# Zero products, landing times and the last step in a kernel whose order is written out

## The chip, the cores and the metric

The kernel runs on one core of a Trainium2 chip. The time is that of the device, in microseconds (us), for one execution; before the change the median of three runs is 809.19 us (808.46 to 811.43).

## The reference

Attention within chunks of 64 tokens (4 batches, 8 heads, 576 tokens, head size 64), and behind it two feed-forward layers over the same 2304 tokens of 512 values, each with 2048 hidden values. The first layer squares its rectified hidden values and applies a scale and an offset; the second is a softplus. All weights of the layers are given as 64-bit floats and are used as 32-bit ones.

```python
scores = scale * np.matmul(q_c, k_c.transpose(0, 1, 2, 4, 3))      # chunks of 64
attn = np.exp(scores - np.max(scores, axis=-1, keepdims=True))
attn = attn / (np.sum(attn, axis=-1, keepdims=True) + 1e-09)
x = np.matmul(attn, v_c)                                           # to 2304 x 512
h = x @ moe_w_in;  r = np.maximum(h, 0.0)
x = (moe_s * (r * r) + moe_b) @ moe_w_out
h = x @ moe2_w_in
return (np.maximum(h, 0.0) + np.log1p(np.exp(-np.abs(h)))) @ moe2_w_out
```

## The kernel before, in words

Attention is done in 18 tiles of 128 tokens (`attention`): scores on TensorE, maximum on VectorE, exponentials on ScalarE, division on GpSimd, a transpose and the product with v on TensorE.

Each of the four matrix products of the layers is computed by a scheme of seven products of half-size blocks in place of eight, with sums of blocks ("forms") made by VectorE and GpSimd. A number is split into a high part, rounded by ScalarE (line 1090), and a low part, the rest, by VectorE (line 1099); a product is then three matmuls (high by high, high by low, low by high) of 128 x 128 weights with 384 columns. All of them have one shape, so a block's product is six matmuls.

A phase is one layer. In its first multiplication (`quad`, matmuls at line 1509) a unit is 256 hidden values by a group of 768 tokens: seven products into four PSUM banks, seeds copied from one bank to the next by ScalarE (line 1531), the nonlinear function on ScalarE (line 1542), and six results stored to DRAM (`summed`). In the second multiplication (`second_by_blocks`, matmuls at line 1952) these are loaded again (`features`, line 1722), split (`divided`), and multiplied with the forms of the second weights. Those forms are made during the first multiplication (`weights2`), spilled to DRAM in eight groups (`spilled`), and loaded by `weights` (line 1663) before their step. One step of the second multiplication is one of the seven products for one of the three groups of tokens: eight products of six matmuls into two banks, three to one bank (`d` = 0) and three to the other (`d` = 1), then `read_out` adds both into the running sums. The last step of the second phase writes the output.

The 32-bit weights come from 64-bit words by integer operations on VectorE and ScalarE (`convert`, lines 956 to 1057).

PSUM has eight banks here: A (2), S (3), at (3). SBUF holds rings of buffers, among them `go` for hidden values on their way to DRAM.

The order of the work is written out. Every operation has a rank in the table `PLAN`, by the name of its turn ("second0 0 1 2 0" is phase 0, product 1, group 2, part 0), with V for VectorE and G for GpSimd where an operation has a choice. `Work.order` (line 669) walks the ranks with assumed durations, one queue to each engine, and gives each operation a planned start and end: a load lands after its bytes at `BYTES` and a constant, `LOAD`, `FIRST` (attention) or `STORE`. The real program is emitted in the order of planned starts; each engine runs its own list in that order and waits on the chip for what it needs. The planned times themselves enter the program at one place only, `warmed` (line 732): where TensorE has a planned gap before an operation, it emits matmuls with an all-zero operand (`nought`, `idle`, line 2075) into a bank that nobody uses. Before, that bank is S2, and no zero product is emitted once S2 is taken for the first time.

All DMAs are issued from one queue (SP, line 918; the loads of attention at line 1286), in the order of the list: a DMA that waits holds those behind it.

Of the kernel before, what the change touches and what calls it, by code (L numbers as in the profile page):

```python
# [19 lines left out]
P = 128  # L20
# [7 lines left out]
NF = NM // 2  # L28
# [48 lines left out]
    "": "0 837 21",  # L77
    "attention 0": "1 2 3 31 12 19 23 25 - 38 42 48 52V 58 64V 68 74",
    "attention 1": "5 6 7 27 22 28 34 41 - 55 60 66 76V 84 106 109 93 95 98 100 108 112",
    "attention 2": "8 9 10 13 37 43 49 56 - 72 75 81 89 107 113 115 121",  # L80
    "attention 3": "20 26 29 85 54 61 70 77 - 90 94 99 104 111 120 128 124 126 132G 130 141 149",
    "attention 4": "33 45 47 91 71 79 86 92 - 110 117 127 131V 135 152 146 156",
    "attention 5": "44 62 69 114 96 102 119 122 - 134 139 147 151 155 164 168 161 166 171 172 175 181",
    "attention 6": "59 63 65 143 88 97 105 133 138 145 153 158 165 174 202 196 205",
    "attention 7": "78 80 82 150 129 142 154 157 163 178 185 190 194 198 206 227 208 210 222G 216G 237 248",
    "attention 8": "101 123 140 184 162 173 177 180 - 197 201 209 215 221 231 229 239",
    "attention 9": "103 116 118 188 169 186 192 199 203 217 226 232 242 249 273 283 256 261 277G 266G 290 305",
    "attention 10": "136 144 148 244 204 213 220 225 230 246 251 259 267 271 279 284 289",
    "attention 11": "170 179 182 240 228 234 245 247 - 264 272 282 288 294 307 314 313 318 323G 321G 380 385",
    "attention 12": "176 183 214 257 243 252 258 262 270 280 285 291 297 302 311",  # L90
    "attention 13": "211 218 238 298 265 275 278 281 286 301 310 333 336 344 359",
    "attention 14": "235 253 255 312 287 295 300 315 - 327 331 340 346 350 363",
    "attention 15": "250 260 263 316 317 322 324 328 332 341 349 356 366 372 383",
    "attention 16": "274 296 304 353 326 334 338 343 347 354 360 368 373 376 386",
    "attention 17": "293 306 309 358 335 345 352 355 361 364 371 375 378 381 392V",
    "held 6": "400 407 390 397 367 402 417 413 411 445 420 442",
    "held 7": "414 427 389 394 391G 415 438 431G 424 449 453 460",
    "held 8": "408 423 395 399 404 412 435 429 418 421 450 456",
    "weights1 0 0": "4 14V 15 18 16 17 24 11 32V 36 39 35 40 46 53 57 30 51G 50 67 73 83",
    "quad0 0 0": "187 191 193 200V 212 233 224 254 268 308 348 236 269 299 276 325 398 320 330 339 369 365 401 342G 377 382 362 406 388",  # L100
    "weights1 0 1": "87 137 160 167 159 189 195 125 219 223 303 241 292 319 351 379 207G 337G 329 357 370 374",
    "quad0 1 0": "387 393 396 405 410 422 419 425 432 437 441 416 426 434 430 439 448 443 457 465 455 458 452 468 470 472 477 474 480",
    "quad0 0 1": "403 433 436 444 447 459 463 467 475 484 492V 461 473 489V 471 502 509 485 493 499 496 500 514 503 506 519 508 512 540",
    "quad0 1 1": "454 476 481 488 491 507 513 518 523 528 534 498 522 531 511 561 571 533 541 545 537 544 572 554 557 562 569 574 566",
    "quad0 0 2": "505 524 527 535 539 551 548 559 564 583 586 546 565 592 563 588 599 570 585 591V 590 594 605 598 604 612 603 609 616",
    "quad0 1 2": "553 568 573 581 584 597 593 602 610 622 632 579 615 620V 608 650 655V 613 625 634 703 624 659 637 639 644G 675 643 649",
    "weights1 0 2": "384 428 446 462 440 451 466 409 469 478 483 479 482 487 575 580 516 497 529 549G 578 582",
    "quad0 2 0": "589 617 621 629 635 640 642 647 653 660 696 638 648 651V 652 657 691 669 679 683 699 673 715 686G 708 724 695 712 866",
    "quad0 2 1": "627 654 656 662 665 672 678 682 690 735 737 689 704 711 676 685 716 694 729 742V 740 717 722 747 753G 761G 756 774 777",
    "quad0 2 2": "595 692 701 709 713 723 728 732 754 748 772 707 731 767V 743 757 768 758 765 770 795 771 791 773 783 818 862 788 848",  # L110
    "weights1 0 3": "611 661V 664 668 663 667 671 645 674V 680 687 681 684 693 698 705 677G 700 697 702 706 710",
    "quad0 3 0": "719 733 738 745 752 766 762 775 781 787 810V 764 776 789V 793 812 826 785 796 799 822 842 831 803 821 830G 807 834 846",
    "quad0 3 1": "727 750 780 794 804 816 813 823 832 861 886 811 819 838 855 902 910V 845 852 856 899 897 939 869 890 895 888 911 919",
    "quad0 3 2": "769 784 800 806 817 825 835 851 863 857 877V 829 864 884 836 854 878 881 889 892 891 967 893 898G 903G 920 916 907 924",
    "weights1 0 4": "726 779V 782 790 786 792 797 763 802 809 814 808 815 824 844 850 805 827 839 843 849 853",
    "quad0 4 0": "860 870 887 896 900 912 917 921 930 935 943 874 909 933 960 982 988 934 941 946V 948 1040 992 953 958G 969 956 980 974",
    "quad0 4 1": "868 875 894 901 904 915 927 947 959 954 957 913 926 931 928 938 945 968 978 1005 976 962 970 1018 1025G 1032 1027 1031 1043",
    "quad0 4 2": "905 929 940 949 952 966 963 975 984 993 997 981 1002 1011 987 1020 1028 991 1000 1007 1001 1033 1096 1021 1035 1041G 1066 1076 1069",
    "weights1 0 5": "859 914V 918 922 925 932 936 908 942V 951 961 944 950 965 973 986 955 979 972G 983 985 989",
    "quad0 5 0": "996 1010 1015 1026V 1029 1036 1039 1044 1052 1047 1048 1022 1038 1068 1050 1060 1109 1057 1065 1072 1054 1073 1112 1078G 1089 1092 1100 1093 1102",  # L120
    "quad0 5 1": "1003 1013 1034 1063 1071 1088 1083 1104 1120 1116 1124 1079 1086 1099 1097 1144 1149V 1126 1136 1140V 1162 1115 1167 1145 1156 1161 1151 1159 1203",
    "quad0 5 2": "1009 1042 1045 1055 1064 1074 1080 1084 1108 1127 1134 1090 1111 1122 1107 1138 1163 1114 1148 1154 1147 1125 1190 1157 1164G 1176 1169 1217 1210",
    "weights1 0 6": "999 1049V 1053 1058 1056 1059 1061 1037 1067V 1077 1082 1070 1075 1085 1091 1105 1087 1098 1095 1103 1106 1110",
    "quad0 6 2": "1119 1129 1132 1141 1146 1155 1165 1174 1186 1192 1196V 1179 1188 1195 1158 1170 1183 1191 1199 1202 1201 1207 1214 1206 1213 1224 1220 1237 1228",
    "weights1 0 7": "1171 1204V 1208 1211 1209 1215 1222 1187 1225 1230 1235 1229 1232 1238 1242 1249 1226 1245 1243 1247 1250 1254",
    "quad0 7 2": "1259 1267 1273 1280V 1284 1293 1297 1310 1319 1332 1337V 1279 1289 1303V 1296 1308 1324V 1323 1329 1342V 1361 1307 1327 1356 1358 1362G 1359 1363 1367",
    "quad0 6 0": "1153 1160 1168 1175 1184 1193 1200 1205 1219 1257 1272 1218 1227 1248 1255 1262 1270 1246 1260 1264V 1278 1268 1276 1269 1275 1283 1274 1281 1287",
    "quad0 7 0": "1302 1311 1317 1325 1328 1340 1336 1349 1360 1390 1394 1357 1366 1371V 1353 1393 1402 1364 1391 1400 1407 1384 1405 1406 1413 1425 1410 1416 1443",
    "quad0 6 1": "1137 1173 1197 1216 1223 1233 1236 1240 1252 1298 1330V 1212 1295 1300 1251 1334 1354 1266 1301 1314 1346 1304 1370 1318G 1333 1350 1412 1386 1381",
    "quad0 7 1": "1291 1316 1335 1339 1341 1372 1355 1379 1395 1428 1434 1399 1432 1439 1404 1440 1462 1411 1437 1453V 1445 1442 1473 1460 1461 1469 1464 1475 1470",  # L130
    "weights2 0 0": "464 490 495 504 494 501 510 486 515 520 525 521 526 532 536 538 542 543G 550 552 556",
    "weights2 0 1": "517 547 555 558 560 567 577 530 587V 601 606 596 600 614 618 623 607 626 636 633 630",
    "weights2 0 2": "576 619 641 646 628 631 658 670 714 720 725 718 721 730 734 736 666 739 746 744 749",
# [5 lines left out]
    "second 0": "1377 1375 1378 1418 1419 1433",  # L139
    "weights 0 1": "1343 1345 1368 1392 1382 1398 1408 1427 1430 1435",  # L140
    "second0 0 1 2 0": "1331 1385 1389 1396",
    "second1 0 1 2 1": "1415",
    "second2 0 1 2 2": "1388 1414 1421",
    "second3 0 1 2 3": "1426",
    "second0 0 1 2 4": "1373 1403 1420 1431",
# [2005 lines left out]
```

## Time and profile before

| what | us |
|---|---|
| three runs | 808.46, 809.19, 811.43 |
| profiled execution | 808.3 |
| its span, first to last instruction | 806.5 |
| TensorE busy with matmuls | 775.9 |
| VectorE busy | 669.8 |
| ScalarE busy | 544.2 |
| GpSimd busy | 116.9 |

The profile shows one execution. PE is TensorE, DVE VectorE, ACT ScalarE, POOL GpSimd, SPq the queue that issues DMAs. Busy time counts from a matmul's start to its modelled end. "PEclk" is the granted clock of TensorE as a share of 2.4 GHz: 0.50 is 1.2 GHz. L2075 are the zero products, L1509 and L1952 the matmuls of the first and the second multiplication. Attention takes the time to about 80 us, the first phase that to about 447 us.

### The profile page before, as it was taken

Reading aid. Unit: us, or ns where it says so; the run is one execution under the profiler, and the core shown is the slowest. Engines: PE = TensorE matmul, PEld = TensorE weight load, DVE = VectorE, ACT = ScalarE, POOL = GpSimd, SP = SyncE. Lnnn points to the kernel's source line nnn. Section 1 sums busy time; section 2 is a strip of 40 time slices with the busy share of each in tenths; the row PEclk is TensorE's granted clock in tenths of the full one; section 3 lists DMA queues with packets and bytes.
Section 4 is the critical chain, followed back from the end, with each engine's and each line's share of the span. In section 5 each row is a group of like instructions: output and inputs, shape, how many; then the busy total and the mean of one; then the engine's idle time right before and its main releaser. Section 6 shows DMA issues by size and latency. Waiting matters only on the chain.

```text
span 806.5 us, 14244 instructions
## 1 busy us (share of the span) xinstructions
PE 775.9 (96%) x4994; PEld 751.0 (93%) x4994; DVE 669.8 (83%) x1193; ACT 544.2 (67%) x1106; POOL 116.9 (14%) x115
## 2 busy tenths in 40 slices
PE   7898899999997999999999999999999999999998
PEld 5687799999996999999999899999999999999997
DVE  5998988998998799898999989999754688666754
ACT  5889897898987687766677865655555455454432
POOL 3355101113112000000001211101022131000000
PEclk8999999999999899999999999999999999999999
DMA  6765478899899989788884068987678987667554
GB/s 235 263 199 174 156 270 260 274 298 313 301 313 320 310 304 329 250 266 288 316 282 159 23 224 271 296 287 257 228 254 283 345 331 239 218 247 243 195 190 177
DMA packets 93658, 205.43 MB, mean 255 GB/s; under 512 B 10001, under 2 KB 64273, under 8 KB 92689
## 3 DMA queue, kind: packets, MB, share of 16 engines
q1 hardware_dynamic: 93584, 204.51, 74.4%
q8 instruction: 39, 0.64, 0.3%
q14 instruction: 35, 0.28, 0.1%
HBM read 128.45 MB, written 76.02 MB: 254 GB/s over the span
## 4 chain that ended last, share of the span: by engine, by line
PE 70%; ACT 9%; DVE 9%; DMA 7%; issue 3%; SPq 1%; POOL 0%; DVEq 0%; ACTq 0%; POOLq 0%
PE at L1509 18%; PE S L1952 12%; PE at L1952 12%; PE S L1509 10%; PE A L1952 7%; PE A L1509 7%; ACT operands L1090 4%; DVE operands L1099 3%; DMA last<-summed 3%; DVE mem L1077 2%; DMA summed<-mem 1%; DMA mem<-summed 1%; DVE last L1077 1%; ACT last L1346 1%; ACT mem L1542 1%
## 5 line engine op out<-in xcount | busy, mean ns | idle before, releaser
L1952 PE MATMUL S<-operands 128*128 128x384 f32 (+1 forms) x768 | 177.2, 337 | 4.5 <-ACT mem L1542 2.8
L1952 PE MATMUL at<-operands 128*128 128x384 f32 (+1 forms) x768 | 175.1, 335 | 0.0
L1099 DVE TENSOR_TENSOR operands<-mem,operands 128x768 fp32r<-128x768 f32 (+2 forms) x147 | 133.2, 925 | 41.2 <-ACT operands L1090 40.7
L1090 ACT CAST operands<-mem 128x768 fp32r<-128x768 f32 (+3 forms) x150 | 115.1, 793 | 70.0 <-PE at L1952 40.6
L1090 ACT CAST operands<-last 128x768 fp32r<-128x768 f32 (+2 forms) x136 | 103.0, 781 | 70.6 <-PE at L1952 33.1
L1952 PEld LDWEIGHTS S<-operands 128*128 128x128 f32 x768 | 136.6, 188 | 7.6 <-DVE operands L1099 4.0
L1077 DVE TENSOR_TENSOR mem<-mem 128x256 f32<-128x256 f32 (+1 forms) x258 | 123.4, 498 | 22.1 <-POOL mem L1077 7.0
L1077 POOL TENSOR_TENSOR mem<-mem 128x256 f32<-128x256 f32 (+1 forms) x72 | 74.3, 1036 | 446.4 <-DVE mem L1077 131.4
L1099 DVE TENSOR_TENSOR operands<-last,operands 128x768 fp32r<-128x768 f32 (+2 forms) x135 | 119.8, 910 | 22.2 <-ACT operands L1090 21.7
L1952 PEld LDWEIGHTS at<-operands 128*128 128x128 f32 x768 | 137.5, 188 | 0.0
L1509 PE MATMUL at<-operands 128*128 128x384 f32 x624 | 120.9, 337 | 4.7 <-ACT S L1531 2.0
L1509 PEld LDWEIGHTS at<-operands 128*128 128x128 f32 x624 | 108.7, 188 | 8.1 <-ACT S L1531 3.4
L1952 PE MATMUL A<-operands 128*128 128x384 f32 (+1 forms) x480 | 89.7, 337 | 1.7 <-DVE operands L1099 1.1
L1952 PEld LDWEIGHTS A<-operands 128*128 128x128 f32 x480 | 83.8, 188 | 3.2 <-DVE operands L1099 2.4
L1509 PE MATMUL S<-operands 128*128 128x384 f32 x420 | 84.3, 340 | 0.0
L1509 PEld LDWEIGHTS S<-operands 128*128 128x128 f32 x420 | 75.3, 192 | 0.4 <-issue 0.2
L1509 PE MATMUL at<-last,operands 128*128 128x384 f32 x336 | 67.8, 339 | 0.0
L1542 ACT ACTIVATE mem<-S 128x384 f32<-128x384 f32 x104 | 50.6, 491 | 24.7 <-PE S L1509 13.3
L1509 PE MATMUL A<-operands 128*128 128x384 f32 x300 | 60.8, 340 | 4.3 <-ACT mem L899 2.7
L969 ACT ACTIVATE mem<-mem 128x512 f32<-128x512 int32 x88 | 55.6, 632 | 8.9 <-DVE mem L960 8.1
L1509 PEld LDWEIGHTS at<-last,operands 128*128 128x128 f32 x336 | 59.5, 188 | 0.3
L1509 PEld LDWEIGHTS A<-operands 128*128 128x128 f32 x300 | 52.0, 188 | 7.2 <-ACT mem L899 3.3
(108 smaller groups left out, 927.3 us busy)
## 6 DMA issues: line engine op xcount, KB each, us to landing
summed<-mem SPq DMA_DIRECT2D x288, 192.0 KB, 3.0
mem<-in_w_dram SPq DMA_DIRECT2D x64, 512.0 KB, 4.7
last<-summed SPq DMA_DIRECT2D x40, 768.0 KB, 5.5
mem<-summed SPq DMA_DIRECT2D x20, 768.0 KB, 5.9
last<-summed SPq DMA_DIRECT2D x28, 384.0 KB, 3.9
last<-in_qk_dram SPq DMA_DIRECT2D x36, 256.0 KB, 3.8
forms<-mem SPq DMA_DIRECT2D x16, 512.0 KB, 4.2
mem<-summed SPq DMA_DIRECT2D x20, 384.0 KB, 6.5
```

Of the source, the lines that this page charges most:

```text
L969: return lambda e: nc.scalar.activation(out=out(), in_=in_(), func=AF.Prelu, scale=scale, bias=bias, alpha=alpha)
L1077: lambda e: on(e).tensor_tensor(out=out(), in0=x(), in1=y(), op=op or ALU.subtract),
L1090: lambda e: nc.scalar.copy(out=hi().bitcast(F32R), in_=x()),
L1099: lambda e: on(e).tensor_tensor(out=lo().bitcast(F32R), in0=x(), in1=hi(), op=ALU.subtract),
L1346: nc.scalar.activation(out=of("e")[:, h * D : (h + 1) * D], in_=at(sc)[:, h * D : (h + 1) * D], func=AF.Exp, scale=SCALE, bias=mx[:, h, 1: ...
L1509: nc.tensor.matmul(acc(dst)().rearrange("p (u c) -> p u c", u=GROUP), l[a], r[c], start=start and kk == 0 and x == 0, stop=kk == 1 and x == 2,
L1542: lambda e: nc.scalar.activation(out=at(go), in_=acc(place)(), func=AF.Softplus if ph else AF.Relu),
L1952: nc.tensor.matmul(at(accs[d])[:, :width], l[a], r[c], start=i == 0 and y == 0 and not seeds, stop=i == NF - 1 and y == 2, skip_group_chec ...
```

## The change

It has five parts. `warmed` looks at every gap of TensorE in the whole program: up to 30 us planned time as before (with at least two zero products before the first operation and four before the second), later only where the planned gap is 1.3 us or more; the bank is the one whose last use ended earliest, and there are none if that was less than 0.5 us before the gap. `FIRST`, `LOAD`, `STORE` and `BYTES` are changed, and the first weights load counts as one of the `FIRST` kind; the table `PLAN` is new in 500 of its lines. A load of spilled weight forms depends on those groups alone that it reads (in the first phase a load takes four of the eight; in the second it takes all). The last step of the second phase does its eight products for `d` = 0 and for `d` = 1 as separate operations of three matmuls, which share their split features (`cut_of`); so `last_of` holds an operation for each `d`, on which `read_out` depends.

```diff
-    "weights 0 1": "1343 1345 1368 1392 1382 1398 1408 1427 1430 1435",
+    "weights 0 1": "1326 1343 1371 1374 1376 1386 1404 1416 1420 1432",
...
-    "sums2 1 2 1": "3595 3597 3594 3596",
+    "second0 1 2 1 0 1": "3564",
...
+    "second3 1 2 1 7 1": "3596",
+    "sums2 1 2 1": "3604 3605 3599 3601",
...
-    STORE, LOAD, FIRST = 2.3, 2.2, 2.9
-    BYTES, TURN = 360e3, 0.6
+    STORE, LOAD, FIRST = 2.7, 2.5, 3.3
+    BYTES, TURN = 357e3, 0.6
...
-        op.lag = self.FIRST if self.part == "attention" else self.LOAD
+        op.lag = self.FIRST if self.part == "attention" or self.turn == "weights1 0 0" else self.LOAD
...
+    EARLY, LONG = 30.0, 1.3
+    FIRST_GAPS = 2, 4
+
+    def warmed(self, done, emit):
+
+        used = {(k, x): [] for k, n in (("S", 3), ("A", 2), ("at", 3)) for x in range(n)}
         for op in done:
-            unused = unused and all((u.kind, u.index) != (kind, index) for u in op.takes)
-            if op.on == "PE" and unused:
+            for u in op.takes:
+                if u.kind in self.BANKS:
+                    used[u.kind, u.index].append((op.start, u.until))
+        t, at, out = 0.0, 0, []
+        for op in done:
+            if op.on == "PE":
                 spare = self.SPARE[op.start < self.CROWDED]
-                for x in range(int((op.start - t - spare) / self.IDLE) if t else 2):
-                    out.append(Op({"PE": self.IDLE}, 0, [], [], [], emit, 0))
+                n = int((op.start - t - spare) / self.IDLE) if t else 0
+                n = max(n, self.FIRST_GAPS[at]) if at < len(self.FIRST_GAPS) else n
+                at += 1
+                if op.start > self.EARLY and op.start - t < self.LONG:
+                    n = 0
+                past = {k: max([b for a, b in v if a <= op.start], default=0.0) for k, v in used.items()}
+                bank = min(past, key=past.get)
+                if past[bank] > t - 0.5:
+                    n = 0
+                for x in range(n):
+                    out.append(Op({"PE": self.IDLE}, 0, [], [], [], lambda e, bank=bank: emit(e, bank), 0))
...
-                        [o for i in range(NF) for o in spilled[ph, i]]
+                        [o for i in range(y * m, y * m + m) for o in spilled[ph, i]]
...
+            elif ph and n == order[-1] and j == groups[2]:
+                products = [(n, i, (d,)) for d in range(2) for i in range(NF)]
+                cut_of = {}
...
+                if ds == (1,):
+                    work.begin(f"second{i % 4}", ph, n, j, i, 1)
+                    pair = cut_of[i // 2]
...
-                    for d in range(2):
+                    for d in ds:
...
-                last_of[n] = add(
-                    {"PE": 6 * mm(width)},
+                o = add(
+                    {"PE": 3 * len(ds) * mm(width)},
```

`SPARE` is 0.4 us and `IDLE`, the planned length of one zero product, 0.24 us; both stay.

## Rows read from the trace of the kernel before

**Rows 1.** the page: engines' busy us, share of the span, instructions; a group of VectorE's

```profile
PE 775.9 (96%) x4994; PEld 751.0 (93%) x4994; DVE 669.8 (83%) x1193; ACT 544.2 (67%) x1106; POOL 116.9 (14%) x115
...
L1099 DVE TENSOR_TENSOR operands<-last,operands 128x768 fp32r<-128x768 f32 (+2 forms) x135 | 119.8, 910 | 22.2 <-ACT operands L1090 21.7
```

**Rows 2.** windows: busy us and instructions by engine, granted clock, DMA share, GB/s

```profile
10.80:17.40 6.60, 5.55 (x27) 4.04 (x26) 4.66 (x13) 6.57 (x37) 2.25 (x2) 0.50 0.77 288
...
260.00:266.60 6.60, 5.33 (x17) 5.33 (x18) 5.91 (x9) 4.75 (x10) 0.00 (x0) 0.50 0.99 336
...
300.00:340.00 40.00, 39.21 (x222) 38.14 (x222) 37.06 (x62) 30.74 (x52) 0.00 (x0) 1.00 0.86 296
...
400.00:440.00 40.00, 40.00 (x232) 40.00 (x231) 38.73 (x65) 30.85 (x50) 6.63 (x6) 1.00 0.74 247
440.00:460.00 20.00, 18.76 (x104) 17.49 (x103) 19.63 (x41) 16.47 (x33) 3.73 (x4) 1.00 0.06 21
```

**Rows 3.** timeline of TensorE, 254 to 269 us: start, us, engine, line, operation, count, [wait before]

```profile
257.38 1.31 PE L1509 MATMUL at<-operands 128*128 128x384 f32 x6 [1.09 <-ACT S L1531]
261.27 1.33 PE L1952 MATMUL S<-operands 128*128 128x386 f32 x3 [2.57 <-ACT mem L1542]
...
263.37 3.82 PE L1509 MATMUL S<-operands 128*128 128x384 f32 x12
```

**Rows 4.** timeline of the DMA queue and of ScalarE, 244 to 262 us

```profile
244.39 1.70 SPq L918 DMA_DIRECT2D forms<-mem  x3
...
248.27 1.42 SPq L918 DMA_DIRECT2D last<-forms  x2
...
255.57 0.49 ACT L1542 ACTIVATE mem<-S 128x384 f32<-128x384 f32 x1 [2.31 <-POOL mem L1077]
...
258.00 2.08 ACT L1090 CAST operands<-last 128x512 fp32r<-128x512 f32 x3
```

**Rows 5.** timeline of TensorE, 9 to 44 us; zero products alone, 10.8 to 17.4 us

```profile
9.54 1.09 PE L1322 MATMUL A<-last 128*64 128x128 f32 x16 [2.39 <-DMA last<-in_qk_dram]
10.56 1.48 PE L2075 MATMUL S<-nought 128*128 128x512 f32 x3
...
42.30 0.96 PE L2075 MATMUL S<-nought 128*128 128x512 f32 x3
43.10 1.21 PE L1509 MATMUL A<-operands 128*128 128x384 f32 x6
...
10.80:17.40 6.60, 3.14 (x7) 1.58 (x6) 0.50 0.77 288
```

**Rows 6.** waits of TensorE: us in total, times, longest us

```profile
PE A L1509 <- ACT mem L899: 2.7, 2, 2.1
...
PE S L1952 <- DVE operands L1099: 1.8, 5, 0.5
...
PE A L1952 <- DVE operands L1099: 1.1, 2, 0.9
```

**Rows 7.** the chain of work in order of time: start, us, what

```profile
93.67 6.71 DMA summed<-mem
...
430.35 8.34 PE A L1952 x48
```

**Rows 8.** DMA issues: count, KB each, median us to landing

```profile
summed<-mem SPq DMA_DIRECT2D x288, 192.0 KB, 3.0
...
out_dram<-last SPq DMA_DIRECT2D x24, 192.0 KB, 2.0
```

**Rows 9.** timeline of all engines at the end

```profile
802.60 0.56 DVE L1077 TENSOR_TENSOR last<-at,last 128x384 f32<-128x384 f32 x1 [3.39 <-PE at L1952]
803.07 0.55 DVE L1077 TENSOR_TENSOR last<-S,last 128x384 f32<-128x384 f32 x1
803.19 0.81 SPq L918 DMA_DIRECT2D out_dram<-last  x2
```

**Rows 10.** timeline of TensorE behind the change of phase

```profile
450.19 3.77 PE L1509 MATMUL at<-operands 128*128 128x384 f32 x18 [0.59 <-ACT S L1531]
```

More of the change, by code (lines that the diff above doesn't have):

```diff
@@ L1838, in read_out @@
                     biased[n, d] = add(
-                        {"DVE": 0.13}, t, f, [o, *scalars, *([biased[1, d]] if n == 2 else [])], [accs[d]]
+                        {"DVE": 0.13}, t, f, [o[d], *scalars, *([biased[1, d]] if n == 2 else [])], [accs[d]]
                     )
@@ L1849, in read_out @@
                             lambda e, dst=dst, ps=ps, x=d: scaled(e, mem(*dst, v), x, ps()),
-                            [o, biased[2, d], *scalars],
+                            [o[d], biased[2, d], *scalars],
                             [accs[d]],
@@ L1858, in read_out @@
                             lambda e, dst=dst, ps=ps: copy(e, mem(*dst, v), ps()),
-                            [o, *(quads_done[0] if not ph and j == groups[0] else [])],
+                            [o[d], *(quads_done[0] if not ph and j == groups[0] else [])],
                             [accs[d]],
@@ L1870, in read_out @@
                             N,
-                            [o],
+                            [o[d]],
                             [accs[d]],
@@ L1918, in second_by_blocks @@
                 z += 1
-            products = [(n, i) for i in range(NF) for n in ns]
+            products = [(n, i, (0, 1)) for i in range(NF) for n in ns]
             if len(ns) > 1:
-                products = [(n, i + x) for i in range(0, NF, 2) for n in ns for x in range(2)]
+                products = [(n, i + x, (0, 1)) for i in range(0, NF, 2) for n in ns for x in range(2)]
+            elif ph and n == order[-1] and j == groups[2]:
+                products = [(n, i, (d,)) for d in range(2) for i in range(NF)]
+                cut_of = {}
             seeds = {n: seeded(n, j, t, accs_of[n]) for n in ns}
-            for y, (n, i) in enumerate(products):
+            for y, (n, i, ds) in enumerate(products):
                 accs = accs_of[n]
@@ L1929, in second_by_blocks @@
                 key = t + y * T
-                if len(ns) > 1:
+                if ds == (1,):
+                    work.begin(f"second{i % 4}", ph, n, j, i, 1)
+                    pair = cut_of[i // 2]
+                elif len(ns) > 1:
                     if i % 2 == 0 and n == ns[0]:
@@ L1938, in second_by_blocks @@
                         pair = divided((a + i % 4 * N, 2 * N), key, ld)
+                if ds == (0,):
+                    cut_of[i // 2] = pair
                 if i == 4 and j == groups[2] and n == ns[-1] and n != order[-1]:
@@ L1959, in go @@
                             )
-                last_of[n] = add(
-                    {"PE": 6 * mm(width)},
-                    key,
-                    go,
-                    [*v2_ready[n, i], *([last_of[n]] if i else seeds[n])],
-                    [*([wp] if wp else []), *accs],
+                o = add(
+                    {"PE": 3 * len(ds) * mm(width)},
+                    key,
+                    go,
+                    [*v2_ready[n, i], *([last_of[n][ds[0]]] if i else seeds[n])],
+                    [*([wp] if wp else []), *(accs[d] for d in ds)],
                     r=[hi, lo, *([spans[i]] if spans[i] else [])],
                 )
+                for d in ds:
+                    last_of.setdefault(n, {})[d] = o
             t += len(products) * T
@@ L2071, in block_attention_two_layers, with idle @@
         make_identity(nc, ident)
-        def idle(e, x=bank["S"][2]):
-            x = x.rearrange("p (a b) -> p a b", b=P)
+        def idle(e, to):
+            x = bank[to[0]][to[1]].rearrange("p (a b) -> p a b", b=P)
             nc.tensor.matmul(x, nought, nought.unsqueeze(1).to_broadcast([P, KK, P]), start=True, stop=True)
-        for x in bank["A"] + bank["S"]:
+        for x in (("A", 0), ("A", 1), ("S", 0), ("S", 1), ("S", 2)):
             idle("PE", x)
-        for op in work.warmed(done, idle, "S", 2):
+        for op in work.warmed(done, idle):
             op.emit(op.on)
```

4 lines of the change are left out of this document (1 added, 3 removed), and 1002 rows, old and new, of the table PLAN.

## The prediction

> **What bounds the kernel now.** I read the page's busy shares first: TensorE is busy for 775.9 us of 806.5 [rows 1], so at full clock only its idle time, its slow time and the two ends are left to win. Then the windows by stage [rows 2]. The granted clock is 1.00 nearly everywhere and 0.50 in two stretches, 10.8 to 17.4 us and 260.0 to 266.6 us. ScalarE fills 6.57 of the 6.60 us of the first. In the second TensorE works at half speed, 5.33 us busy of 6.60, and no other engine is full. VectorE is close behind TensorE from 300 to 340 us (37.06 of 40), from 400 to 440 (38.73 of 40) and in the change of phase (19.63 of 20). Next the timeline of TensorE where the first multiplication ends and the second begins [rows 3]: it waits 1.09 us, runs six matmuls, waits 2.57 us, and 1.3 us into that wait the clock falls to the 1.2 GHz level; there twelve matmuls take 3.82 us. Behind the last wait stands ScalarE, which splits weights just before it [rows 4]. Last the list of TensorE's waits [rows 6] and the chain [rows 7], for waits that end with a late DMA.
>
> The profiled execution took 808.3 us, 1.8 more than its span. The three runs are 808.46, 809.19 and 811.43; the lower two, which agree to 0.1%, have their mean at 808.8. I sum against 808.3 and carry the difference to 808.8.
>
> **Zero products late in the program.** Before, they stop when bank S2 is first used, the last of them at 42.30 us [rows 5]; from 255 to 268 us TensorE has none. Now the gap before the first product of the second multiplication can be filled: by the formula in the change, a planned gap of 2.57 us would get (2.57 - 0.4) / 0.24 = 9 products, and at (43.10 - 42.30) / 3 = 0.27 us each [rows 5] they take 2.4 us, less than the wait. If they hold the clock, the 5.33 us of work at half speed [rows 2] shrink by half: 2.66 us. The bounds are 0 and 2.66. Part is given back: VectorE has 2.9 us to spare from 300 to 340, 1.3 from 400 to 440 and 0.4 in the change of phase [rows 2]. But part of VectorE's work there waits for TensorE and moves with it. I take four fifths, **-2.1**.
>
> The price is a zero product in a gap that the plan sees and the chip does not have. In the list of ranks the last product of the first multiplication and the first of the second lie 17 places apart before and 29 after, since three more products of the last unit now run ahead of the gap instead of behind it; at 3598 operations in 806.5 us, 4.5 a microsecond, the planned gap is long and its zero products many, but what they fill is the same wait, moved. The place to fear is the change of phase: there the ranks lie 11 apart before and 12 after, so a gap may be planned; the chip shows a wait of 0.59 us a little behind that place [rows 10] and none at it. Four zero products would take 4 x 0.27 = 1.1 us, of which 0.59 may come out of that wait. Bounds 0 and +1.1; I take **+0.3**, since TensorE would come to it earlier than before and so nearer to the plan.
>
> **Fewer and other zero products early.** The second product of TensorE now has four ahead of it, 4 x 0.27 to 4 x 0.49 us (three took 1.48 at the low clock), inside a wait of 2.39 us for a load [rows 5]. That may hold the clock from 10.8 us on. But ScalarE has 0.03 us free in that stretch [rows 2] and the attention tiles behind it need ScalarE, so a faster TensorE mostly waits longer. Five zero products between 35 and 43 us go where gaps are under 1.3 us; the three at 42.30 are 0.8 us in all. Bounds -1.2 (half of what is busy in the stretch and no zero product, 5.55 - 3.14 us [rows 2, 5]) and +0.5; I take **-0.2**.
>
> **Half of the spilled weights is enough for half of a load.** The last three stores of forms are issued from 244.39, the two loads of the next weights from 248.27 [rows 4]. The first load needs only the first four stored groups now, and its rank falls from 1343 to 1326, so it can go 17 / 4.5 = 3.8 us earlier. ScalarE sat idle 2.31 us before 255.57 and three casts of the loaded weights, 2.08 us, run from 258.00, shortly before the PSUM reads (L1542) that TensorE's 2.57 us wait ends with [rows 3, 4]. One such cast is 2.08 / 3 = 0.69 us; two of them could move into the idle time, 1.4 us. Bounds 0 and -2.3 (the whole idle time); the new list puts other PSUM reads between, so I take **-0.8**. What this shortens, zero products no longer need to fill.
>
> **An order computed with later landings.** 137 of 726 TensorE operations, 295 of 627 of the queue and about half of ScalarE's and VectorE's leave the longest common order; 48 go from VectorE to GpSimd and 47 back, 41 from VectorE to ScalarE and 30 back. Nothing is added, so the work is the same to about 11 operations. It can remove waits that a late DMA made: 2.1 us at 101 us behind a store of 6.71 us, 1.8 us in five waits of the second multiplication, 0.9 us in one wait near the end [rows 6, 7], 4.8 us in all. It can also make as many new ones: bounds -4.8 and +4.8. An allowance that is larger by 0.2 to 0.4 us is small beside a landing of 6.71, so I count on a third, **-1.5**.
>
> These rows also show that landing follows load: 192 KB take 2.0 us at the end and 3.0 in the median elsewhere [rows 8], 6.71 in the worst place [rows 7]. An allowance that is the same everywhere is then too long in one place and too short in the other, which is rival E below.
>
> The Trainium skill ("DMA: Bandwidth & Descriptors", section Latency and other measured facts) says of the fixed cost that it is mostly HBM's latency, low on average and several times higher at high load. The rows agree in direction; by that rule the order's term is nothing and the sum is 1.5 us nearer to zero.
>
> **The last step in two halves.** Before, both accumulators end together: VectorE adds at 802.60 and again from 803.07, and two stores are issued in 0.81 us [rows 9]. Now one half is read out while the other still multiplies, with three half products still to start after that read-out by the ranks (3600, 3602 and 3603 after 3599). One add (0.47 us) goes from the end, and half of the issues (0.4 us). Bounds -0.9 and +0.9, if the last pair of features, which is needed earlier, is late by one VectorE pass of 910 ns [rows 1]. I take **-0.7**. The count of matmuls and weight loads is the same.
>
> Sum: -2.1 + 0.3 - 0.2 - 0.8 - 1.5 - 0.7 = -5.0: 803.3 for the profiled execution, **803.8 us** against 808.8.
>
> **Rivals.** (A) VectorE and ScalarE become the bound: TensorE runs through 260 to 268 at full clock and waits the same time at 300 to 340 and in the change of phase. For it: VectorE's 0.4 us of slack there and the waits for its operands [rows 2, 6]; against it: the chain into the change of phase runs on TensorE for 8.34 us from 430.35 [rows 7]. Then -0.4 for the clock, +0.3, -0.7, -0.2 and -0.5 for the order: 807.3. (B) The change does not do what it says: no bank is free in the long gap, or zero products come too late and the clock falls at the same place. Two units of the first multiplication are open there, with four accumulators each, and TensorE has eight banks. Then the first two terms are 0: 808.8 - 0.2 - 0.8 - 1.5 - 0.7 = 805.6. (C) Slower: loads that start earlier push the stores of the first multiplication back; its buffers come free late and ScalarE, then TensorE, wait as at 101 us, 2.1 us each time [rows 6, 7]. The DMA share from 260 to 266.6 is already 0.99 [rows 2]. Four such waits are 8.4 us; with the gains of clock and end (-2.8) that is 814.4. It decides from four waits on; two make 810.2. Against it: in the whole list ScalarE's copies make one wait of that length, though the share is high for long stretches [rows 2, 6]. (D) The order removes most of its 4.8 us and the transition gives its 2.3: 808.8 - 2.1 - 0.2 - 2.3 - 4.0 - 0.7 + 0.3 = 799.8. (E) Landing follows load and the order brings nothing, neither gain nor new wait: 808.8 - 3.5 = 805.3. For it, the spread of 2.0 to 6.71 us [rows 7, 8]; against it, that the five waits of the second multiplication are short, 1.8 us together, and an allowance of 0.3 us each would cover most of them.
>
> **How the numbers follow.** About 0.5% (4.0 us) is what a measurement of this kernel can tell from no change: faster is under 804.8 here, slower over 812.8. Forecast 0.40 (0.36 faster, 0.04 same), A 0.16 (same), B 0.12 (0.03 faster, 0.09 same), C 0.10 (slower), D 0.10 (faster), E 0.12 (0.04 faster, 0.08 same). That makes faster 0.53, same 0.37, slower 0.10. The range of 799.0 to 810.5 takes in A, B, E and most of D, and the mild form of C; what it leaves out is C and the end of the order's bounds on the good side.
>
> **What would show it.** Right: zero products in the trace near 255 us, a granted clock of 1.00 there, twelve matmuls in 2.1 us; one VectorE add behind the last matmul; waits for ScalarE and VectorE operands in 300 to 350 us that are no longer than before. Wrong: a second stretch at 0.50 as before (B); VectorE busier than 97% in 300 to 340 and new waits on it (A); TensorE's total idle time in 80 to 230 us, with zero products not counted as work, above that of before (C).

## The result and the profile after

The changed kernel takes 800.81 us (median of 4 runs, 799.44 to 801.83), the kernel before beside it 808.87: the ratio is 0.9893, interval 0.9866 to 0.9920. That is 8.1 us less by the medians, where 5.0 were forecast; the time lies in the range of 799.0 to 810.5. Run once more on another occasion it took 799.42 beside 808.14, ratio 0.9892 (0.9849 to 0.9935).

The profiled execution took 799.44 us, its span is 797.6. The windows, to compare with [rows 2] (the first two lines are the start; the third and fourth the end of the first multiplication):

```profile
7.20:10.80 3.60, 3.51 (x23) 2.30 (x23) 3.20 (x7) 3.57 (x18) 0.00 (x0) 1.00 1.02 397
10.80:17.40 6.60, 5.62 (x74) 4.16 (x75) 6.53 (x17) 6.44 (x35) 4.00 (x3) 1.00 0.86 327
...
256.00:260.00 4.00, 3.58 (x17) 2.70 (x16) 2.99 (x7) 4.00 (x9) 2.48 (x3) 1.00 0.94 343
260.00:266.60 6.60, 6.48 (x35) 5.93 (x34) 6.60 (x11) 5.32 (x10) 0.00 (x0) 1.00 0.82 248
300.00:340.00 40.00, 38.88 (x224) 38.44 (x222) 35.40 (x61) 30.24 (x52) 1.68 (x2) 1.00 0.87 288
...
400.00:440.00 40.00, 40.00 (x233) 40.00 (x232) 39.13 (x68) 35.02 (x60) 4.75 (x5) 1.00 0.64 214
440.00:460.00 20.00, 19.49 (x110) 18.79 (x109) 19.93 (x44) 15.71 (x32) 1.88 (x2) 1.00 0.17 61
```

Both stretches at 0.50 are gone. TensorE's timeline at the places of [rows 3], [rows 5] and [rows 10], L2108 being the zero products now, L1532 and L1983 the two multiplications:

```profile
6.99 1.80 PE L2108 MATMUL S<-nought 128*128 128x512 f32 x4
8.73 1.09 PE L1345 MATMUL A<-last 128*64 128x128 f32 x16
...
39.33 1.32 PE L1532 MATMUL A<-operands 128*128 128x384 f32 x6
...
252.81 2.24 PE L1532 MATMUL S<-operands 128*128 128x384 f32 x12
254.89 1.20 PE L1532 MATMUL A<-operands 128*128 128x384 f32 x6
255.93 3.15 PE L2108 MATMUL at<-nought 128*128 128x512 f32 x13
258.91 0.33 PE L1983 MATMUL S<-operands 128*128 128x386 f32 x1
...
260.13 0.69 PE L1983 MATMUL at<-operands 128*128 128x386 f32 x3
...
263.82 1.32 PE L2108 MATMUL at<-nought 128*128 128x512 f32 x5
...
440.30 1.77 PE L2108 MATMUL S<-nought 128*128 128x512 f32 x7
441.91 5.39 PE L1532 MATMUL at<-operands 128*128 128x384 f32 x30
```

The wait of 2.57 us is filled with 13 zero products in bank at. Behind them three matmuls take 0.69 us in place of 1.33 [rows 3]; the twelve that took 3.82 us there now run ahead of the gap and take 2.24. Five more zero products stand at 263.82 and seven at the change of phase. The first product of the first layer starts at 39.33 us in place of 43.10 [rows 5]. The end, to compare with [rows 9]:

```profile
792.01 2.24 PE L1983 MATMUL S<-operands 128*128 128x384 f32 x12
792.20 0.56 DVE L1100 TENSOR_TENSOR last<-at,last 128x384 f32<-128x384 f32 x1 [2.73 <-PE at L1983]
794.29 0.56 DVE L1100 TENSOR_TENSOR last<-S,last 128x384 f32<-128x384 f32 x1 [1.52 <-PE S L1983]
```

One half is added 2.1 us before the other. From the last matmul's end to the end of the span it is 3.39 us (794.25 to 797.64), before 3.95.

So the zero products, the clock and the halves came as described. What each is worth is another question, since the lead over the kernel before does not grow where the parts are. The table has the starts of matmuls by their number (counted from 0, in the order in which TensorE runs them) in four profiles: "before", the table of ranks alone with the loads that go with it, the changed kernel, and its second profile. All are in us:

| matmul | before | table alone | after | again |
|---|---|---|---|---|
| first of the first layer | 43.10 | 41.60 | 39.33 | 39.79 |
| 900th of its first multiplication | 239.54 | 238.57 | 235.45 | 235.69 |
| 96th of its second | 283.83 | 280.70 | 277.92 | 278.82 |
| 432nd | 345.32 | 339.73 | 336.37 | 339.26 |
| 864th | 421.87 | 417.46 | 415.34 | 415.82 |
| 100th of the second layer | 466.55 | 462.41 | 460.13 | 460.60 |
| end of the last one | 802.56 | 796.35 | 794.25 | 794.14 |

### The profile page after: what moved, and what is told of

It is laid out like the page before. It is cut to its first block, busy times and chain, and to the rows that moved or that the text cites. A ratio compares the mean times of both kernels' runs of the same rounds, so it can differ in the third digit from the quotient of the medians.

```text
span 797.6 us, 14301 instructions
## 1 busy us (share of the span) xinstructions
PE 775.0 (97%) x5017; PEld 750.8 (94%) x5017; DVE 670.7 (84%) x1181; ACT 553.8 (69%) x1117; POOL 118.8 (15%) x116
## 4 chain that ended last, share of the span: by engine, by line
PE 70%; DVE 13%; DMA 7%; ACT 6%; issue 3%; POOL 1%; SPq 0%; DVEq 0%; ACTq 0%; POOLq 0%
PE at L1532 19%; PE S L1983 12%; PE at L1983 12%; PE S L1532 10%; PE A L1983 8%; PE A L1532 6%; DVE operands L1122 5%; DMA last<-summed 3%; DVE mem L1100 2%; DMA summed<-mem 2%; ACT last L1369 2%; ACT operands L1113 1%; PE at L1466 1%; DVE mem L1066 1%; DVE mem L1080 1%
## 5 line engine op out<-in xcount | busy, mean ns | idle before, releaser
L1983 PE MATMUL S<-operands 128*128 128x384 f32 (+1 forms) x768 | 175.7, 336 | 2.2 <-ACT operands L1113 1.1
L1983 PE MATMUL at<-operands 128*128 128x384 f32 (+1 forms) x768 | 173.9, 334 | 0.0
L1122 DVE TENSOR_TENSOR operands<-mem,operands 128x768 fp32r<-128x768 f32 (+2 forms) x148 | 135.6, 935 | 36.9 <-ACT operands L1113 36.6
L1100 POOL TENSOR_TENSOR mem<-mem 128x256 f32<-128x256 f32 (+1 forms) x78 | 82.9, 1067 | 485.7 <-DVE mem L1100 236.5
L1983 PEld LDWEIGHTS S<-operands 128*128 128x128 f32 x768 | 136.1, 188 | 5.0 <-DVE operands L1122 2.8
L1983 PEld LDWEIGHTS at<-operands 128*128 128x128 f32 x768 | 136.9, 188 | 0.0
L1100 DVE TENSOR_TENSOR mem<-mem 128x384 f32<-128x384 f32 (+1 forms) x252 | 124.1, 510 | 13.9 <-ACT mem L1565 4.5
L1532 PE MATMUL at<-operands 128*128 128x384 f32 x624 | 120.0, 336 | 1.6 <-ACT S L1554 0.8
L1532 PEld LDWEIGHTS at<-operands 128*128 128x128 f32 x624 | 108.8, 188 | 3.9 <-ACT S L1554 1.1
L1983 PE MATMUL A<-operands 128*128 128x384 f32 (+1 forms) x480 | 90.0, 336 | 0.2
L1983 PEld LDWEIGHTS A<-operands 128*128 128x128 f32 x480 | 83.7, 188 | 1.2 <-DVE operands L1122 1.1
L1532 PE MATMUL S<-operands 128*128 128x384 f32 x420 | 82.8, 335 | 0.0
L1532 PEld LDWEIGHTS S<-operands 128*128 128x128 f32 x420 | 73.6, 188 | 0.4 <-issue 0.2
L1532 PE MATMUL at<-last,operands 128*128 128x384 f32 x336 | 67.6, 338 | 0.4 <-DVE mem L1100 0.4
L992 ACT ACTIVATE mem<-mem 128x512 f32<-128x512 int32 x88 | 55.5, 631 | 11.8 <-DVE mem L983 10.8
L1532 PE MATMUL A<-operands 128*128 128x384 f32 x300 | 61.2, 341 | 2.3 <-ACT S L1554 1.5
L1532 PEld LDWEIGHTS at<-last,operands 128*128 128x128 f32 x336 | 59.5, 188 | 0.8 <-DVE mem L1100 0.7
L1532 PEld LDWEIGHTS A<-operands 128*128 128x128 f32 x300 | 51.7, 188 | 5.8 <-ACT S L1554 3.3
```

The costliest lines, as they stand in the source:

```text
L992: return lambda e: nc.scalar.activation(out=out(), in_=in_(), func=AF.Prelu, scale=scale, bias=bias, alpha=alpha)
L1100: lambda e: on(e).tensor_tensor(out=out(), in0=x(), in1=y(), op=op or ALU.subtract),
L1122: lambda e: on(e).tensor_tensor(out=lo().bitcast(F32R), in0=x(), in1=hi(), op=ALU.subtract),
L1532: nc.tensor.matmul(acc(dst)().rearrange("p (u c) -> p u c", u=GROUP), l[a], r[c], start=start and kk == 0 and x == 0, stop=kk == 1 and x == 2,
L1983: nc.tensor.matmul(at(accs[d])[:, :width], l[a], r[c], start=i == 0 and y == 0 and not seeds, stop=i == NF - 1 and y == 2, skip_group_chec ...
```

## The experiments

Times are medians; the kernel before ran beside each (808.21, 808.37 and 808.14 us in the three sets; its single runs lie between 804.4 and 812.8). A ratio is the kernel's time over that of the kernel before beside it, with its 95% interval in brackets. Each experiment has one profile. An edit shifts line numbers, so in each profile the same operations stand at other lines.

**The order alone.** The kernel before with the new table and the loads by groups; zero products, landing constants and last step as before.

```diff
 PLAN = {
-    ...                  # in words: the ranks of before
+    ...                  # those of after, without the eight turns of the last step's second half
...
-                        [o for i in range(NF) for o in spilled[ph, i]]
+                        [o for i in range(y * m, y * m + m) for o in spilled[ph, i]]
```

> The kernel before with the new table of ranks and the loads that depend on four groups, and nothing else: old rule for zero products (none late, none of the four), old landing constants, whole products in the last step. Theory O (the order is the gain; zero products and halves are worth about 1.5 us together): 802.0 (6 below before). Rival Z (zero products at the start and late carry half of it): 804.3 or more, the first product at 41.5 or later.

802.42 us, ratio 0.9917 (0.9891 to 0.9943): 6.0 us less by the medians. Theory O holds. Its clock falls at both places, at the start for 6.8 us as before, at the transition for 3.4 us in place of 6.8, and its first product comes at 41.60:

```profile
10.50:17.30 6.80, 6.19 (x34) 4.42 (x34) 4.92 (x14) 6.77 (x38) 2.27 (x2) 0.50 0.92 353
263.10:266.50 3.40, 3.40 (x12) 3.40 (x12) 3.40 (x7) 2.48 (x4) 0.00 (x0) 0.50 1.05 298
```

So of 8.1 us some 6 are the order; for zero products, halves and constants together about 2 stay, and the two intervals overlap. No run here divides those 2 us among the parts: each part that was left out below left the time of the changed kernel within the noise.

**The order in two parts.** Operations whose rank is under 2170 in both tables (up to the change of phase) keep the old order and the rest gets the new, and the reverse.

```text
in words, for each operation:
first kernel:  rank of before where both ranks are under 2170, else that of after
second kernel: rank of after where both ranks are under 2170, else that of before
```

> The kernel before with its own order for the operations up to the change of phase (those whose rank is under 2170 in both tables) and the new order behind them; nothing else is changed. The table alone is worth 6.0 us in all, and of that 1.6 us lie behind 460 us in the two profiles. Theory: TensorE has no wait behind 460 us (0.00 to 0.02 us in every profile of the new table, 0.19 to 1.30 with the old) and the kernel takes 1 to 2 us less than before beside it. Rival (the waits there come from what the first layer leaves behind): waits of 0.2 us or more behind 460, no gain.

> The complement: the new order up to the change of phase with loads that depend on four groups, the old order behind it; no late zero products, none of the four, whole products. Theory: 4 to 5 us less than before beside it, the first product of the first layer at 41.6, that of the second multiplication's second hundred (the 96th matmul) at 280.7, and waits of 0.2 to 1.3 us behind 460 us. Rival (the two parts of the order are worth something only together): less than 2 us.

New behind: 806.95 us, ratio 0.9986 (0.9962 to 1.0010). New ahead: 803.19, ratio 0.9934 (0.9911 to 0.9957). By the medians 1.2 and 5.0 us, together 6.2 beside the 6.0 of the whole table; the first is inside its noise. The first product of the second kernel comes at 40.72, earlier than the 41.6 expected; its clock was at 0.50 for 3.4 us at the start. The waits of TensorE from 460 to 800 us in the second kernel are nearly those of before (two of 1.1 us in all, [rows 6]):

```profile
PE A L1952 <- DVE operands L1099: 1.3, 2, 1.0
```

The first kernel has none in that stretch. In all eight profiles with the new order there TensorE waits 0.00 to 0.02 us, in all six with the old 0.19 to 1.31.

**Late zero products.** Left out of the changed kernel, and put alone into the kernel before.

```diff
-    EARLY, LONG = 30.0, 1.3
+    EARLY, LONG = 30.0, 1e9         # the changed kernel without them
-        for op in work.warmed(done, idle, "S", 2):
+        for op in work.warmed(done, idle):     # the kernel before with them, FIRST_GAPS = 2, 0
```

> The changed kernel without its zero products behind 30 us. Theory (they hold the clock): the granted clock is 0.50 for some 6.6 us from about 257 us on, the ten products there take twice as long, and the kernel takes 803.0 us (800.8 + 2.7 for the clock - 0.5 for the seven zero products left out at the change of phase). Rival (the new order alone moved the gap, the clock would hold without them): clock 1.00 throughout and 800.2 us.

> The kernel before with the new rule for zero products alone, without the four at the start: the old order. Theory: about ten of them before 261.27 us, clock 1.00 there, 2.1 us won at 293 us and kept to the end but for up to 1 us at the change of phase: 806.3 us. Rival A of the prediction: the clock holds, but VectorE's operands take the gain back by 350 us: 808.3. Rival B: the clock falls all the same: 808.8.

Without them: 800.55 us, ratio 0.9902 (0.9875 to 0.9930), the changed kernel's time within the noise. The clock does fall, as the theory says; the windows of this kernel:

```profile
259.30:266.10 6.80, 6.06 (x18) 5.66 (x19) 6.39 (x11) 5.51 (x10) 0.33 (x1) 0.50 1.00 316
```

Against the changed kernel it is 0.66 us behind at the 900th matmul, 2.0 at the 96th of the second multiplication: 1.3 us lost here. At the 720th of that multiplication it is 0.3 us behind (389.71 against 389.45), at the 100th of the second layer 1.6 again, and 1.0 at the end: the lead comes and goes. The theory's time fails, its 803.0 us lie above every run (798.49 to 800.95). Nor is the 1.3 us sure: from the 900th matmul to the 96th the four profiles with the 13 zero products take 42.3 to 43.3 us, the four with the new order there and without them 42.1 to 43.8. By time, the 16 runs of kernels with the 13 have a mean of 800.1 us, the eight of changed kernels without them (this one, and the one below with all groups) 799.8. Where the lead of this pair goes at first: the changed kernel waits 1.12 us before 339.73 and 0.56 before 340.72, and the chain that leads there is that of two loads:

```profile
324.00 4.57 DMA last<-summed
...
332.91 5.85 DMA last<-summed
...
338.85 0.84 ACT operands L1113
...
339.71 0.97 DVE operands L1122
...
340.72 0.62 PE S L1983 x2
```

In the kernel before with the late rule, 806.80 us, ratio 0.9993 (0.9976 to 1.0011), the rule put nothing into the long gap:

```profile
257.59 1.33 PE L1525 MATMUL at<-operands 128*128 128x384 f32 x6 [1.09 <-ACT S L1547]
261.47 1.34 PE L1968 MATMUL S<-operands 128*128 128x386 f32 x3 [2.56 <-ACT mem L1558]
```

and the clock fell at 259.7 us. Its zero products stand at 228.6, at 292.1 and at 447.7 us. That is rival B's outcome in the old order, where three products of the last unit run behind the gap. Which condition of the rule stopped it follows from the plan, worked out from this kernel's own table: it has a gap of 2.91 us there, room for ten zero products, but the bank whose last use ends earliest is in use until 2.0 us into the gap. So it is the condition on the bank, as rival B had it. In the plan of the changed kernel the gap is 3.73 us, and a bank is free 1.7 us before it.

**Four zero products at the start.** Left out of the changed kernel, and put alone into the kernel before.

```diff
-    FIRST_GAPS = 2, 4
+    FIRST_GAPS = 2, 0               # the changed kernel
+                n = 4 if at == 1 else n     # in warmed of the kernel before
```

> The changed kernel with the four zero products ahead of TensorE's second operation left out. The first product of the first layer comes at 39.33 us now and came at 43.10 before. Theory L (the new order of the first loads made this): it stays within 0.7 us of 39.33, and the time within 0.7 of 800.8, whatever the clock does. Theory C (the clock at the start made it): the clock is 0.50 for 6.8 us from about 11 us, the first product comes at 42 or later, and the kernel takes 803 or more.

> The kernel before with four zero products ahead of TensorE's second operation and nothing else: the old order. Theory C (the clock at the start is worth the 3.8 us): clock 1.00 from 8 to 20 us, first product of the first layer near 40 us, 805.3 us. Theory L (the order of the loads is): the first product at 42.5 or later, 808 us, clock or not.

Without them: 800.56 us, ratio 0.9907 (0.9883 to 0.9930). With them in the kernel before: 807.13, ratio 0.9990 (0.9970 to 1.0010). Neither time differs from its parent's. The first product comes at 40.92 in the first (clock at 0.50 for 3.4 us) and at 42.31 in the second (clock never at 0.50 there), so both theories named a part: about 0.8 us of the start is the clock in the old order, by one profile each. In the new order the first product comes at 41.60 with 6.8 us at 0.50, at 40.72 to 41.12 with 3.4 us (three profiles), and at 39.33 to 40.65 with the clock held (four). The order alone is worth 1.5 us of the 3.8; of the rest a part is the clock and a part differs from one execution to the next. The four do not hold the clock every time. Of seven profiles with them it fell once, of seven without them it held once. The case where it fell, with TensorE waiting 1.91 us behind them:

```profile
6.55 1.20 PE L2108 MATMUL S<-nought 128*128 128x512 f32 x4
9.66 1.97 PE L1345 MATMUL A<-last 128*64 128x128 f32 x16 [1.91 <-DMA last<-in_qk_dram]
```

**The first loads.** Two moves in the DMA queue of the kernel before, without and with the four zero products.

```diff
-    "attention 2": "8 9 10 13 37 ...
+    "attention 2": "9 10 11 32 37 ...
-    "weights1 0 0": "4 14V 15 18 16 17 24 11 32V ...
+    "weights1 0 0": "4 14V 15 18 16 17 24 8 32V ...
```

> The kernel before with two changes in the list of the DMA queue: the second load of the first weights goes ahead of the loads of attention tile 2, and the load of that tile's v goes behind the loads of tile 3 and 4. Theory L (these loads hold up the scores of tiles 2 and 3, and ScalarE behind them): the first product of the first layer comes 2.0 us earlier (43.1 to 41.1) and the kernel takes 806.2 (2.0 less than the 808.2 of before beside it). Rival (ScalarE and VectorE set the pace of attention, or the new list's other moves did it): the first product within 0.5 us of 43.1, time within noise of before.

> The same two moves of loads and four zero products ahead of TensorE's second operation, in the kernel before. If the start of the changed kernel is these two things, the first product comes at 39.9 (39.33 there, 43.10 before; the four alone gave 42.31) and the kernel takes 805.2. If they overlap (both only bring the scores of tile 2 forward), it comes at 41 and the time is that of the loads alone. If it stays above 42, the rest of the new order of attention made the start.

807.64 us, ratio 0.9995 (0.9969 to 1.0020), and 809.50, ratio 1.0004 (0.9979 to 1.0028): no gain. Their first products come at 41.46 and 41.59 us, 1.6 and 1.5 earlier than before, so a part of the new start is these loads. But the clock held in both, and beside the 42.31 of the four alone the loads bring 0.7 to 0.85. What became of the 1.6 us is plain in the profile of the first of the two: a load of features landed 7.89 us after its issue and TensorE waited for what was made of it,

```profile
334.28 7.89 DMA last<-summed
```

```profile
344.14 0.80 PE L1952 MATMUL S<-operands 128*128 128x384 f32 x2 [3.17 <-DVE operands L1099]
```

and the clock was at 0.50 for 3.4 us from 344.4. After that the kernel is 1.9 us behind the kernel before at the 576th matmul (373.15 against 371.23), having been 3.5 ahead at the 288th. The second kernel has no such wait; its lead is 0.4 us at the 288th (318.00 against 318.42).

**The last step in halves.** The changed kernel with whole products.

```diff
-            elif ph and n == order[-1] and j == groups[2]:
+            elif False:
```

> The changed kernel with its last step as eight whole products again. Theory: VectorE adds twice behind the last matmul and two stores follow, 0.5 to 0.9 us longer at the end: from the last matmul to the end of the span 3.9 us in place of 3.4, 801.4. Rival: the store's landing sets the end, the second add hides in it, and the time is that of the changed kernel within 0.2.

800.28 us, ratio 0.9881 (0.9845 to 0.9916). The two adds stand one behind the other again:

```profile
794.94 0.56 DVE L1100 TENSOR_TENSOR last<-at,last 128x384 f32<-128x384 f32 x1 [4.81 <-PE at L1983]
795.42 0.55 DVE L1100 TENSOR_TENSOR last<-S,last 128x384 f32<-128x384 f32 x1
795.53 0.81 SPq L941 DMA_DIRECT2D out_dram<-last  x2
```

and from the last matmul to the end it is 3.95 us, against 3.38 or 3.39 in each of the five profiles with halves (the others with whole products have 3.94 to 3.96, the order alone 4.24). The mechanism is shown, 0.56 us, at the low end of what the theory gave; the time of the whole kernel cannot show it.

**Loads by groups, and the changed kernel again.** Each load waiting for all eight groups; the other is unchanged.

```diff
-                        [o for i in range(y * m, y * m + m) for o in spilled[ph, i]]
+                        [o for i in range(NF) for o in spilled[ph, i]]
```

> The changed kernel with each load of spilled weights waiting for all eight groups again. Theory (the prediction's -0.8): the first load of the second multiplication's weights goes out some 3 us later, the casts behind it too, the first product of the second multiplication at 260 or later against 258.91, and the kernel takes 801.6. Rival (the order is made for the earlier load and ScalarE's list is held up by it): 2 us or more, 803. Other rival: nothing, within 0.5 of 800.8.

> The changed kernel once more, unchanged, beside the three others. If its start at 39.33 us and its full clock were a matter of that one execution, this profile has the first product of the first layer between 39.3 and 41.2 and perhaps 3.4 us at 0.50 near 10 us; from 255 to 268 us the clock should be 1.00 again. Time 800.8 within 0.8.

799.62 us, ratio 0.9895 (0.9843 to 0.9946), and 799.42, ratio 0.9892 (0.9849 to 0.9935): the second rival, nothing. The queue shows why. With all groups and in the changed kernel alike the load goes out 0.09 us behind the last store of forms, which stands before it in the list:

```profile
244.73 1.13 SPq L941 DMA_DIRECT2D forms<-mem  x1
245.95 1.08 SPq L941 DMA_DIRECT2D last<-forms  x1
```

```profile
242.56 1.18 SPq L941 DMA_DIRECT2D forms<-mem  x1
243.83 1.00 SPq L941 DMA_DIRECT2D last<-forms  x1
```

From there to the first product of the second multiplication it is 14.85 us with all groups and 15.08 with four (258.91 - 243.83). The kernel with all groups also lost the 13 zero products of the long gap, since its planned times moved, so it is a second test of those. Here is its transition, and the same place of the unchanged one:

```profile
257.03 1.20 PE L1532 MATMUL A<-operands 128*128 128x384 f32 x6
260.80 0.45 PE L1983 MATMUL S<-operands 128*128 128x386 f32 x1 [2.57 <-ACT operands L1113]
```

```profile
255.83 1.20 PE L1532 MATMUL A<-operands 128*128 128x384 f32 x6
256.87 3.15 PE L2108 MATMUL at<-nought 128*128 128x512 f32 x13
259.85 0.33 PE L1983 MATMUL S<-operands 128*128 128x386 f32 x1
```

Its clock was at 0.50 for 3.4 us from 262.1. It is 1.9 us behind already at the 900th matmul of the first multiplication (237.63 against 235.69), 2.4 at the 96th of the second (281.21 against 278.82), 0.7 at the 432nd, and 0.3 ahead at the 576th (365.41 against 365.71); it has no wait from 270 to 440 us, the other has these:

```profile
PE S L1983 <- DVE operands L1122: 1.6, 2, 1.1
PE A L1983 <- DVE operands L1122: 0.4, 1, 0.4
```

Both end their last matmul at 794.2 (794.20 and 794.14). The lead was turned into waits.

## Why the prediction was right, and where its sum was not

The direction and the range held; the sum was put together from the wrong parts. That it came out on the right side of no change owes something to luck: five of its six terms, -3.5 us together, brought little that the time shows, and one, put at -1.5, brought 6.0.

- **An order computed with later landings, -1.5: the term that was mis-sized.** Table and loads by groups measured -6.0 by the medians (ratio 0.9917, 0.9891 to 0.9943), and the loads by groups alone nothing, so the table is worth four times the term and by the medians more than the bound of 4.8, which the interval takes in. I counted the waits of TensorE that a late DMA had visibly made and took a third. The first two columns of the table above show where the lead of the order alone stands: 1.5 us at the first product, 1.0 at the 900th, 3.1 at the 96th, 5.6 at the 432nd, 4.4 at the 864th, 4.1 in the second layer and 6.2 at the end. Two of these places the count leaves out. One is the start (43.10 to 41.60 us with the clock at 0.50 for 6.8 us in both), where ScalarE is full (6.77 of 6.80 us) and a table can still bring 1.5 us. The other is the transition, 2.2 us between the 900th matmul and the 96th of the second multiplication (283.83 - 239.54 against 280.70 - 238.57). There the clock is low for 3.4 us in place of 6.8, and that may be all of it: the two old-order kernels with 3.4 us take 42.5 and 43.2 us for the stretch, three new-order ones with 3.4 us 42.1 to 43.6. That the order makes the low stretch shorter is not shown. The last part lies behind 460 us, where the count had 0.9 us in one wait; in every profile with the new order all waits there are gone.
- **Zero products late, -2.1: mechanism right, worth wrong.** The clock held, and at most 1.3 us were won at the place, in one pair of profiles. To the end nothing that can be measured comes through (800.55 without, 800.81 and 799.42 with). The step that failed is that the 5.33 us at half speed shrink by half: once the clock holds, VectorE is full in that stretch (6.60 of 6.60 us from 260.0, where it had 5.91 before [rows 2]), and TensorE has room for five more zero products at 263.82. What is won goes back in waits behind loads that land 4.57 and 5.85 us after their issue. That is the outcome of rival A for this one term but not its mechanism: from 300 to 340 us VectorE is busy for 35.40 of 40, less than before (37.06).
- **The price at the change of phase, +0.3: nothing.** The seven zero products took 1.77 us, and the kernel without them is no faster there: from the 864th matmul to the 100th of the second layer 44.79 us with them and 45.60 without (416.17 to 461.77). VectorE is full there, 19.93 of 20 us from 440.
- **Start, -0.2: nothing that the time shows.** The clock is worth about 0.8 us at the first product in the old order; by the time that the whole kernel takes, neither the kernel with the four alone nor the one without them shows it.
- **Half of the spilled weights, -0.8: nothing.** The step that failed is that the wait for all eight groups holds the load up. It goes out behind the last store of forms either way, by its place in the list. The kernel with all groups is 0.95 us later at the first product of the second multiplication (260.80 against 259.85), but it was 1.9 us late before that load mattered.
- **Halves, -0.7: 0.56.**
- **Rivals.** C did not come: the table made no set of new waits (TensorE is idle for 3.1 us from 80 to 230 us, before for 5.5). B came in the old order only. D's total, 799.8, is nearest, and its -4.0 for the order too; that the total fits is in part luck, since its -2.1 for zero products and -2.3 for the transition did not come as such. E, by which the order brings nothing, is refuted: landings do spread (4.57 to 7.89 us for three loads of 384 KB), and a table with 0.3 us more allowed for each still took 6 us off. Why so small an allowance does it is open: the new table came out of a new computation, and no run here separates the constants from what a second computation with the old ones would have found. The planned times also enter the program at a second place beside `warmed`: `Work.order` gives each operation the buffer that is free first by the plan. No run tests what that does.

## What to carry to other kernels

In a program with a fixed order, a lead won at one place is worth what the next late load leaves of it. Follow the start times of the same instructions through both profiles before a local gain is put into a sum. Waits with a name show only a part of what a new order can give; try the order alone first. And look at several profiles of one kernel: the first of the changed kernel was 3.8 us ahead at the start, and up to 2.3 us of that went with a clock that holds in some executions only (41.60 with the order alone, 39.33 to 40.65 where it held).

## What was not expected of the hardware

Before the first rise of the clock the page shows 1.00, but the 16 score matmuls at 5.09 us take 1.97 us as at 0.50, against 1.09 at 8.73: the early shares cannot be the granted clock. That they take 1.97 us at 0.50 is shown by the same 16 at 9.66 us above, in the kernel where the clock fell.

The length of one wait does not tell whether the clock falls. At the same place of the first multiplication, behind the same six matmuls, TensorE waits 1.78 us in the kernel with the new order behind the change of phase, and the clock goes to 0.50 at 231.7 us for 3.4 us. In the kernel before with the four zero products it waits 2.31 us there, and the clock stays at 1.00:

```profile
231.13 1.88 PE L1509 MATMUL at<-operands 128*128 128x384 f32 x6 [1.78 <-DVE mem L1077]
```

```profile
230.96 1.33 PE L1512 MATMUL at<-operands 128*128 128x384 f32 x6 [2.31 <-DVE mem L1080]
```

Runs of the changed kernel lie between 798.3 and 801.8 us (eight), those of the kernel before between 804.4 and 812.8 (64). That the new order makes them scatter less is not shown by so few.
